# Up-projection of the last three token chunks of an attention-plus-feed-forward kernel by seven block products instead of eight

## The chip, the cores and the metric

The kernel runs on one core of a Trainium2 chip. A core has a matrix engine (TensorE, PE in the profile; its weight loads are listed as PEld), a vector engine (VectorE, DVE), a scalar engine (ScalarE, ACT), GpSimd (POOL) and SyncE (SP), which here only issues transfers. Each engine executes its own queue of instructions in order, and engines wait for each other by semaphores. The metric is device time in microseconds (us) of one execution.

## What is computed

The inputs are q, k and v (8 batches, 8 heads, 576 tokens, 64 elements) and two weight matrices.

```python
scores = scale * np.matmul(q, k.transpose(0, 1, 3, 2))      # scale = 1/8
# heads 0-3: a query sees the last 32 tokens; heads 4-7: every 4th of the last 128
attn = softmax of the masked scores
x = np.matmul(attn, v), heads side by side                   # 4608 tokens x 512
h = x @ w_in                                                 # 512 -> 2048
g = np.maximum(0.01 * h, h)                                  # leaky ReLU
out = g @ w_out                                              # 2048 -> 512, float32
```

## The kernel before

Every engine's order is written by a planner. The kernel makes a list of tasks (`add`, line 68; `dma`, line 74), each with an engine or a choice of engines, an assumed duration and latency, its dependencies and a priority, and `run` (line 85) simulates the engines and sorts the tasks by planned start. The instructions are issued in that order, so each engine's order is fixed when the program is built; at run time an engine waits wherever something it needs is late. Dependencies between instructions are found again from the memory that they touch when the program is built, and become semaphore waits.

**Attention.** Batches are taken in order, two at a time (a pair is `m`). For late batches scores are made on PE (lines 891, 898), the exponential is on ACT (line 910), the mask is a multiplication on DVE (line 924), the product with the values is on PE (line 931), and DVE takes reciprocals and normalizes (lines 949, 953). PE transposes the result (line 979), and ACT or DVE copy it to `xt` (line 560 or 562), which holds x with its 512 features as four blocks of 128 partitions and 1152 tokens of the pair along the free dimension. Tokens stand there in the order of attention's blocks: token 4t + r stands at r times a block length plus t. DVE also transposes q and k (lines 592, 603), and POOL converts and rearranges.

**Feed-forward.** The 4608 tokens are 12 chunks of 384 (`chunks`, line 501), three to a pair: the first 384 tokens of either batch, and the last 192 of both. For the last pair the order is first batch, both remainders, second batch, which are chunks 9, 10 and 11. *Up* (`up`, line 997) makes one of 16 blocks j of 128 hidden units for a chunk: four matmuls (line 1014), one for each 128 input features, with a 128x128 block of w_in as the stationary operand and 384 tokens moving. They add up in one of two PSUM banks (`hps`), and ACT applies the leaky ReLU (Prelu) as it copies the bank to `gt` in float16 (line 1025). *Down* is done plainly for the first 8 tiles of 128 tokens (`down`, line 1055) and for the other 28 in groups of four tiles (`group`, line 1105): a 2x2 block product made of seven block products in place of eight, with sums of blocks of w_out (line 1095) and of g (line 1139) made by DVE, products on PE (line 1153), and results taken out of PSUM by ACT (line 1182) and added by DVE (line 1190). These use the banks `fps`; the last group also uses four others, among them `sps0`, `tp` (called `tpf` in the code) and `ops`, which belong to attention before.

**Stores.** Since the tokens of a chunk are not in their natural order, `rows` (line 1033) splits a tile of 128 tokens into runs whose output rows lie four apart, and `store` (line 1049) issues one transfer for each run on SP's queue. In the last group the second and later runs of a tile go on ACT's queue.

**Order around the change.** An up task's priority comes from the chunk's due time (`begins`, line 506) and j. In the last stage PE alternates ups of chunks 9 to 11 with the down products of the groups. The last up of chunk 11 is followed by the last group alone.

Of the kernel before, what the change touches and what calls it, by code (L numbers as in the profile page):

```python
# [11 lines left out]
AF = mybir.ActivationFunctionType  # L12
ALU = mybir.AluOpType
# [48 lines left out]
class _Plan:  # L62
# [5 lines left out]
    def add(self, eng, dur, lat, deps, fn, prio, soft=0.0, kind=""):  # L68
        choices = eng if isinstance(eng, tuple) else ((eng, dur),)
        t = _Task(choices, lat, deps, fn, prio, soft, len(self.tasks), kind)  # L70
        self.tasks.append(t)
        return t
# [70 lines left out]
def kernel(  # L143
# [10 lines left out]
    nc = tc.nc  # L154
# [3 lines left out]
    B, H, S, D = q.shape  # L158
    assert (B, H, S, D) == (8, 8, 576, 64)
    DM = H * D  # L160
    DFF = moe_w_in.shape[1]
    NP = H // 2
    NI = DM // 128
    NJ = DFF // 128
# [8 lines left out]
    N_UPS = 8  # L173
# [11 lines left out]
    def at(tl, p0, p1, off, *dims):  # L185

        row = tl.ap[0][0]
        return bass.AP(tensor=tl.tensor, offset=tl.offset + p0 * row + off,
                       ap=[[row, p1 - p0]] + [list(d) for d in dims])

    def dram(t, off, *dims):
        return bass.AP(tensor=t.tensor, offset=t.offset + off, ap=[list(d) for d in dims])
# [7 lines left out]
    w_in = sbuf("w_in", [128, NI * DFF])  # L200
    w_out = sbuf("w_out", [128, NJ * DM])
    NST, NNAT, NVS, NV, NT, NE, NR, NO, NG, NL = 5, 3, 3, 3, 6, 4, 4, 3, 3, 2
    PAD = 32
    stg = [sbuf(f"stg{i}", [128, 1152], FP32) for i in range(NST)]
# [4 lines left out]
    vp = [sbuf(f"vp{i}", [128, 12 * 128]) for i in range(NV)]  # L209
    vd = [sbuf(f"vd{i}", [128, 16 * 128]) for i in range(NV)]  # L210
# [9 lines left out]
    xt = [sbuf(f"xt{i}", [128, NI * 1152]) for i in range(2)]  # L220
    gt = [sbuf(f"gt{i}", [128, NJ * 384]) for i in range(NG)]
# [16 lines left out]
    sps0, tpf = bank("sps0"), bank("tp")  # L238
    tpb = tpf.bitcast(FP16)
    ops = [bank(f"ops{i}") for i in range(2)]  # L240
    hps = [bank(f"hps{i}") for i in range(2)]
# [7 lines left out]
    add = plan.add  # L249
# [29 lines left out]
    rings = {}  # L279
# [185 lines left out]
    w_in_t, w_out_t = {}, {}  # L465
# [35 lines left out]
    chunks = [(m, i, 384) for m in range(B // 2) for i in ((0, 1, 2) if m < 3 else (0, 2, 1))]  # L501
# [4 lines left out]
    begins = [0.0]  # L506
# [7 lines left out]
    def columns(c, x, n):  # L514

        i = chunks[c][1]
        if i < 2:
            return S * i + x, [[1, n]]
        return (384 + S * (x // 192) + x % 192,
                [[1, n]] if x % 192 + n <= 192 else [[S, n // 192], [1, 192]])  # L520
# [31 lines left out]
    x_done, x_free = {}, {1: w_used[14] + w_used[15]}  # L552
# [444 lines left out]
    def up(c, j, x, n, done, acc):  # L997

        m, _, n_c = chunks[c]
        x0, dims = columns(c, x, n)  # L1000
        if c == 0 and j in WIDE:
            h_users = []
            ht, name, x_r = {2: (fps[1], "F", -1), 3: (banks["S"][0], "S", -1), 4: (ops[0], "O", 0),
                             5: (ops[1], "O", 1), 6: (tpf, "TP", -1)}[j]
            h_old = rings[name][x_r]
            rings[name][x_r] = h_users
        else:
            hn, h_old = ring("H", len(hps), h_users := [])
            ht = hps[hn]

        def pe(i0, i1):
            def fn(e):
                for i in range(i0, i1):
                    nc.tensor.matmul(ht[:, 0:n],  # L1014
                                     at(w_in, 0, 128, i * DFF + j // 2 * 256 + j % 2, [2, 128]),
                                     at(xt[m % 2], 0, 128, i * 1152 + x0, *dims),
                                     start=(i == 0), stop=(i == NI - 1))
            return fn
        t_p = None
        for i0, i1 in [(i, i + 1) for i in range(NI)] if c == 0 and j in BLOCKS else [(0, NI)]:  # L1020
            t_p = add("PE", (i1 - i0) * (0.0026 + n * 0.000417), 0.25 * (i1 == NI),
                      done + w_in_t[j][:i1] + h_old + [t_p], pe(i0, i1),
                      begins[c] + j * 1.3 - 6.0 * (c == len(chunks) - 1), 0.0, "U")
        t_a = add("ACT", 0.06 + n * 0.00085, 0.22, [t_p] + gt_free.get(c - NG, []),
                  lambda e: nc.scalar.activation(  # L1025
                      out=gt[c % NG][:, j * n_c + x:j * n_c + x + n], in_=ht[:, 0:n],
                      func=AF.Prelu, alpha=0.01),
                  -1000 + c * 16 + j)
        h_users.append(t_a)
        acc[j].append((t_a, x, n))  # L1030
        return t_p

    def rows(c, tt):

        m, i, _ = chunks[c]
        res = []
        for p in range(128):
            x = columns(c, tt * 128 + p, 1)[0]
            for b in (2 * m, 2 * m + 1):
                for u0, nu, base in segs[b]:  # L1040
                    if base <= x < base + 4 * nu:
                        tok = b * S + 4 * (u0 + (x - base) % nu) + (x - base) // nu
            if res and tok == res[-1][1] + 4 * res[-1][2]:
                res[-1][2] += 1
            else:
                res.append([p, tok, 1])
        return res

    def store(ob, i, c, tt, c0, n_o, t_c, users, both=False):
        for n_p, (p0, tok, n) in enumerate(rows(c, tt)):  # L1050
            users.append(load("ACT" if both and n_p else "SP",
                              dram(out, tok * DM + c0, [4 * DM, n], [1, n_o]),
                              ob[p0:p0 + n, i:i + n_o], n, 4 * n_o, [t_c], -3000))

    def down(c, tt, acts, at_time):
# [44 lines left out]
        minus(3, w_block(0, 1), w_block(1, 1), w_block(0, 1), [t_sum[1]] + plain_parts)  # L1100

    last_of = {}
    SUMS = 75.0

    def group(four, acts, at_time, split):

# [14 lines left out]
        if split:  # L1121
            cells = [[(b, 0) for b in pair] for pair in (fps, [sps0, tpf], ops)]
            pairs = ((0,), (1,))
            room = {id(b): last_of[id(b)] for b in fps}
            room.update({id(b): rings["S2"][-1] for b in (sps0, tpf)})
            room.update({id(b): sum(rings["O2"][-2:], []) for b in ops})
        else:
            cells = [[(b, HN * i) for i in range(2)] for b in (*fps, fps[1])]
            pairs = ((0, 1),)
            room = {id(b): last_of.get(id(b), first_banks.get(id(b), [])) for b in fps}  # L1130
        X, Y, Z = cells
# [185 lines left out]
    for m in range(B // 2):  # L1317
        for b in (2 * m, 2 * m + 1):
            if b < EARLY:
                attend(b, 0, *RANKS[2 * b])  # L1320
                if b == 0:
                    release()
                    first_acts = [[] for _ in range(NJ)]
                    first_ups = [up(0, j, 0, 384, x_done[0, 0], first_acts) for j in range(N_UPS)]
                    clear_slots(range(4, NT), -700, x_done[0, 0][-1:])
                    clear_ones((2,), x_done[0, 0][-1:])
                attend(b, 1, *RANKS[2 * b + 1])
            else:
                a, z = WHEN[b - 1], WHEN[b]
                attend(b, None, a, (z - a) / 4)  # L1330
        x_free[m + 2] = first_ups if m == 0 else []
        while n_c < len(chunks) and chunks[n_c][0] == m:
            acts = first_acts if n_c == 0 else [[] for _ in range(NJ)]
            halves = [(0, 192), (192, 192)] if m == 0 and n_c % 3 == 2 else [(0, 384)]
            for i, (x, n) in enumerate(halves):
                x_free[m + 2] += [up(n_c, j, x, n, x_done[n_c, i], acts)
                                 for j in range(0 if n_c else N_UPS, NJ)]
            gt_free[n_c] = []
            all_acts[n_c] = acts
            for i, (c, tt) in enumerate(tiles[:PLAIN]):  # L1340
                if c == n_c:
                    down(c, tt, [[t for t, x, n in a if x < tt * 128 + 128] for a in acts],
                         begins[c + 1] + tt * 6.92 + 0.6)
            if n_c == 2:
                weight_sums()
                half_free[0] = [t for e in (visits[b, vi, 1][1] for b in range(EARLY)
                                            for vi in range(4)) for t in e]
                half_free[0] += sum((visits[1, vi, 1][2] for vi in range(4)), [])
                part_free[0] = part_free[1] = rings["STG"][-1]
                for i in range(2):  # L1350
                    first_banks[id(fps[i])] = rings["F"][i - 2]
            for n, four in enumerate(groups):
                if four[-1][0] == n_c:
                    group(four, all_acts, begins[n_c + 1] + four[-1][1] * 2.0, n == len(groups) - 1)
            n_c += 1
# [59 lines left out]
```

## Time and profile before

| what | us |
|---|---|
| median of 3 runs | 310.16 (309.3 to 310.33) |
| the profiled execution, own time | 311.24 |
| its span, first to last instruction | 309.5 |
| PE busy | 297.8, 96% of the span |
| DVE, ACT, POOL busy | 204.3, 178.7, 126.1 |
| mean granted PE clock | 0.997 |
| last DVE instruction ends | 304.75 |

The profile is of one execution on the chip. The page has the busy time of each engine, the span in 40 slices, the chain of work that ended last, followed back from the last instruction, and the costliest groups of instructions by line, shape and tile. Queries of the trace give further views: a timeline (start, duration, engine, line, operation), waits (who waited for whom, total, times, longest), and windows (busy time of each engine in a stretch). In a group, "gt<-hps 128x384 f16<-128x384 f32 x171" means 171 instructions that write gt from hps with those shapes; behind the bar stand the busy us, the mean ns of one and the idle time before them with what ended it. Times in a timeline count from the start of the span.

### The profile page before, as it was taken

The page shows a single profiled execution, that of the slowest core. Times are in us where ns is not written, and L with a number is a line of the kernel's source. Part 1 is how long each engine was busy: PE and PEld are TensorE (multiplying, and loading weights), DVE is VectorE, ACT ScalarE, POOL GpSimd, SP SyncE. Part 2 cuts the span into 40 slices and gives each one's busy share as a digit, 9 for nine tenths or more (in the row PEclk, how much of TensorE's full clock was granted, in tenths as well). Part 3 has the DMA queues.
Part 4 walks back from the last instruction along what each step waited for, and adds up shares of the span by engine and source line. Part 5 has one row for each costly group of instructions (what it writes and reads, how often), then busy time and mean ns, then how long its engine had stood idle before and what let it go on. Part 6 is the DMA issues. An engine that isn't in the chain of part 4 may idle for free.

```text
span 309.5 us, 7405 instructions
## 1 busy us (share of the span) xinstructions
PE 297.8 (96%) x2795; PEld 214.1 (69%) x2795; DVE 204.3 (66%) x419; ACT 178.7 (58%) x426; POOL 126.1 (41%) x178
## 2 busy tenths in 40 slices
PE   7987999999999999999999999999999999999993
PEld 2534645567777777787777878787887767777882
DVE  5854896689786859969798798967645230070551
ACT  3736775786556678465776665556545655445320
POOL 4449555475675639268645671961000000000000
PEclk9999999999999999999999999999999999999998
DMA  7999998999899999985999978793103010310133
GB/s 245 314 333 401 397 355 152 223 216 222 235 179 221 210 167 192 167 206 123 193 179 181 194 153 193 137 201 80 36 22 84 6 30 2 84 51 2 36 100 105
DMA packets 163188, 51.25 MB, mean 166 GB/s; under 512 B 140752, under 2 KB 160080, under 8 KB 163152
## 3 DMA queue, kind: packets, MB, share of 16 engines
q1 hardware_dynamic: 162128, 50.05, 68.1%
q10 hardware_dynamic: 1024, 0.73, 0.9%
q8 instruction: 22, 0.36, 0.5%
q14 instruction: 14, 0.11, 0.1%
HBM read 41.32 MB, written 9.44 MB: 164 GB/s over the span
## 4 chain that ended last, share of the span: by engine, by line
PE 87%; DMA 4%; DVE 3%; SPq 3%; ACT 1%; issue 1%; DVEq 0%; ACTq 0%
PE hps L1014 38%; PE fps L1153 25%; PE fps L1066 9%; PE ops L931 3%; DMA wst<-in_moe_w_in_dram 3%; SPq L263 3%; PE ops L979 2%; DVE ee L924 1%; DMA stg<-in_k_dram 1%; PE ops L1153 1%; PE tp L610 1%; PE sps L891 1%; PE tp L891 1%; PE sps L898 1%; PE tp L898 1%; ACT gt L1025 1%
## 5 line engine op out<-in xcount | busy, mean ns | idle before, releaser
L1014 PE MATMUL hps<-xt,w_in 128*128 128x384 f16 (+1 forms) x812 | 144.3, 313 | 1.4 <-DVE w_in L273 0.7
L1025 ACT ACTIVATE gt<-hps 128x384 f16<-128x384 f32 (+1 forms) x203 | 93.7, 468 | 69.9 <-PE hps L1014 67.9
L1014 PEld LDWEIGHTS <-w_in 128*128 128x128 f16 x832 | 75.2, 98 | 37.7 <-DVE w_in L273 1.5
L1153 PEld LDWEIGHTS <-gt 128*128 128x128 f16 x672 | 64.7, 98 | 12.0
L597 POOL COPY slots<-turned 64x576 f16<-64x576 f16 x48 | 35.5, 740 | 51.5 <-DVE turned L592 46.8
L1153 PE MATMUL fps<-w_out,gt 128*128 128x256 f16 x416 | 53.6, 273 | 0.0
L273 POOL CAST nat<-stg 128x576 f16<-128x576 f32 (+1 forms) x53 | 38.2, 745 | 7.5 <-DMA stg<-in_q_dram 2.7
L1066 PE MATMUL fps<-w_out,gt 128*128 128x512 f16 x128 | 32.4, 379 | 0.0
L1190 DVE TENSOR_TENSOR osb<-fps,stg 128x512 f32<-128x512 f32 x18 | 12.4, 688 | 28.0 <-ACT stg L1182 19.0
L953 DVE TENSOR_TENSOR rc<-ops,recs 96x384 f16<-96x384 f32 x48 | 25.8, 541 | 0.3
L1182 ACT COPY stg<-fps 128x512 f32<-128x512 f32 (+1 forms) x24 | 12.8, 532 | 13.2 <-PE fps L1153 11.8
L273 POOL CAST vd<-v_all 128x1024 f16<-128x1024 f32 (+2 forms) x20 | 18.0, 918 | 5.5 <-DMA v_all<-in_v_dram 5.3
L949 DVE RECIPROCAL recs<-ops 96x6 f32<-96x6 f32 x48 | 8.9, 185 | 17.2 <-PE ops L931 15.0
L924 DVE TENSOR_TENSOR ee<-ee,con 128x576 f16<-128x576 f16 x24 | 16.7, 699 | 3.8 <-ACT ee L910 3.7
L562 DVE COPY slots<-tp 64x128 f16<-64x128 f16 (+7 forms) x43 | 13.8, 334 | 8.0 <-PE tp L610 7.4
L592 DVE STREAM_TRANSPOSE turned<-nat 128x576 f16<-128x576 f16 x24 | 17.9, 755 | 0.0
L1066 PEld LDWEIGHTS <-gt 128*128 128x128 f16 x128 | 11.5, 98 | 9.1
L603 DVE STREAM_TRANSPOSE slots<-nat 128x576 f16<-128x576 f16 x24 | 17.6, 749 | 0.0
L924 DVE TENSOR_TENSOR el<-el,con 128x576 f16<-128x576 f16 x24 | 15.7, 656 | 2.1 <-ACT el L910 2.1
L273 POOL CAST vp<-v_all 128x768 f16<-128x768 f32 x16 | 15.4, 970 | 3.3 <-DMA v_all<-in_v_dram 2.1
L1139 DVE TENSOR_TENSOR gt<-gt 128x1024 f16<-128x1024 f16 x19 | 12.9, 692 | 3.8 <-PE fps L1153 3.7
L776 ACT ACTIVATE ee<-sps 128x384 f16<-128x384 f32 x20 | 9.8, 490 | 8.6 <-PE sps L770 5.7
(120 smaller groups left out, 399.6 us busy)
## 6 DMA issues: line engine op xcount, KB each, us to landing
stg<-in_q_dram SPq DMA_DIRECT2D x48, 144.0 KB, 3.8
stg<-in_k_dram SPq DMA_DIRECT2D x48, 144.0 KB, 2.9
v_all<-in_v_dram SPq DMA_DIRECT2D x24, 256.0 KB, 3.5
v_all<-in_v_dram SPq DMA_DIRECT2D x24, 192.0 KB, 2.9
gt<-in_moe_w_in_dram SPq DMA_DIRECT2D x5, 512.0 KB, 8.1
out_dram<-osb SPq DMA_DIRECT2D x24, 96.0 KB, 2.0
out_dram<-osb SPq DMA_DIRECT2D x36, 48.0 KB, 1.8
out_dram<-osb SPq DMA_DIRECT2D x25, 64.0 KB, 2.1
```

The costliest lines, as they stand in the source:

```text
L273: ENG[e].tensor_copy(out=dst, in_=src)
L562: nc.vector.tensor_copy(out=dst, in_=src)
L592: lambda e: nc.vector.transpose(xb, na[:, 0:S]), prio)
L597: lambda e, p0=p0, hh=hh: nc.gpsimd.tensor_copy(out=at(qb, p0, p0 + 64, hh * S + o, *od), in_=at(xb, p0, p0 + 64, i, *id_)), prio, 0.0, "m ...
L603: lambda e: nc.vector.transpose(kb[:, PAD:PAD + S], na[:, S:2 * S]), prio)
L924: nc.vector.tensor_tensor(out=x, in0=x, in1=mk, op=ALU.mult)
L953: nc.vector.tensor_tensor(out=at(xb, 0, 96, 768 * n + 64 * i, [256, 3], [128, 2], [1, D]), in0=at(ot, 0, 96, 0, [130, 3], [65, 2], [1, D]) ...
L1014: nc.tensor.matmul(ht[:, 0:n], at(w_in, 0, 128, i * DFF + j // 2 * 256 + j % 2, [2, 128]), at(xt[m % 2], 0, 128, i * 1152 + x0, *dims), st ...
L1025: lambda e: nc.scalar.activation(out=gt[c % NG][:, j * n_c + x:j * n_c + x + n], in_=ht[:, 0:n], func=AF.Prelu, alpha=0.01),
L1066: nc.tensor.matmul(ft, g[:, j * n_c + tt * 128:j * n_c + tt * 128 + 128], w_out[:, j * DM:j * DM + DM], start=(j == 0), stop=(j == NJ - 1))
L1139: lambda e: nc.vector.tensor_tensor(out=dst, in0=a, in1=b, op=op),
L1153: nc.tensor.matmul(bk[:, x:x + HN], tl[:, off + j * step:off + j * step + 128], rhs(j), start=first and x == 0 and j == 0, stop=j == HJ - ...
```

## The change

Chunks 9, 10 and 11 (`FAST`) are projected up by `up_fast` in place of `up`. Their product x times w_in is seen as 2x2 blocks: input features in two halves k, hidden units in two halves n, tokens in two halves y of 192. A quarter p takes two j of either half of the hidden units (four blocks j in all, of 16), and makes its eight block products by seven, each of four matmuls of 192 columns (two j, two input blocks).

- `w_in_sums` makes four sums of blocks of w_in on DVE: three go to `vd`, whose values are no longer needed, and the fourth overwrites a block of w_in after the last plain up.
- For each chunk four differences of blocks of x are made on DVE (`less`) in a slot of `vp`.
- A quarter uses two banks, X and Y, of a ring of three pairs: `hps`; `sps0` and `tp`; `ops`. Products 1, 6, 5 and 3 add up in X, with a copy of X to a slot of `stg` by ACT or DVE (`evict`) after each of the first three. Products 2, 7 and 4 are made in Y, and DVE adds Y to a copy (`plus`).
- Each of the four results goes through the leaky ReLU on ACT (`relu`), three of them from the copies in `stg` and one from X. It writes g in token order: the elements of a residue are written four apart.
- `rows` gives such chunks their natural token order, so a tile has one run, or two where it crosses from one batch's remainder to the other's.

```diff
+    def up_fast(c, done, acc):
+            up_ring.append([[(hps[0], hps[1]), rings["H"][-1] + rings["H"][-2]],
+                            [(sps0, tpf), rings["S2"][-1]],
+                            [ops, rings["O2"][-1] + rings["O2"][-2]]])
...
+        less(1, b(0, 1), b(0, 0), done + old)
+        less(2, b(1, 1), tx[1], [t_x[1]])
+        less(3, b(1, 1), b(0, 1), done + old)
+        less(4, b(1, 0), tx[2], [t_x[2]])
...
+            def product(k, lhs, rhs, cell, first, deps):
+                def pe(e):
+                    for z in range(2):
+                        for i in range(2):
+                            nc.tensor.matmul(cell[:, n * z:n * z + n], lhs(2 * p + z, i), rhs(i),
+                                             start=first and z == 0 and i == 0,
+                                             stop=z == 1 and i == 1, skip_group_check=True)
...
+            p1 = product(0, raw(0, 0), x_raw(0, 0), X, True, done + w_all + room)
+            p2 = product(1, raw(1, 0), x_raw(1, 0), Y, True, done + w_all + room)
+            e1 = evict(0, [p1] + room_k)
+            a11 = plus(0, [e1, p2])
+            r11 = relu(keep[0], 0, 0, [a11])
+            p6 = product(2, summed(1), x_sum(2), X, False, [e1, t_x[2], w_in_sum[2]])
+            p7 = product(3, raw(0, 1), x_sum(3), Y, True, [a11, t_x[3], w_in_sum[3]])
+            e2 = evict(1, [p6] + room_k)
+            p5 = product(4, summed(0), x_sum(1), X, False, [e2, t_x[1], w_in_sum[1]])
+            e4 = evict(2, [p5] + room_k)
+            a22 = plus(2, [e4, p7])
+            r22 = relu(keep[2], 1, 1, [a22])
+            p3 = product(5, summed(2), x_raw(1, 1), X, False, [e4, w_in_sum[4]])
+            p4 = product(6, raw(1, 1), x_sum(4), Y, False, [a22, t_x[4]])
+            r12 = relu(X[:, 0:2 * n], 0, 1, [p3])
+            a21 = plus(1, [e2, p4])
+            r21 = relu(keep[1], 1, 0, [a21])
...
     def rows(c, tt):
+        if c in FAST:
+            x = tt * 128
+            if i < 2:
+                return [(0, (2 * m + i) * S + x, 128, 1)]
...
-            users.append(load("ACT" if both and n_p else "SP",
-                              dram(out, tok * DM + c0, [4 * DM, n], [1, n_o]),
+                              dram(out, tok * DM + c0, [step * DM, n], [1, n_o]),
...
+    SUMS, IN_SUMS = 75.0, 190.0
+    FAST = (9, 10, 11)
...
+                if n_c in FAST:
+                    up_fast(n_c, x_done[n_c, i], acts)
+                    continue
```

## Prediction

> **What bounds the kernel now.** I read the page first: the share of busy time by engine, the slices, and the chain that ended last.
>
> ```profile
> span 309.5 us, 7405 instructions
> PE 297.8 (96%) x2795; PEld 214.1 (69%) x2795; DVE 204.3 (66%) x419; ACT 178.7 (58%) x426; POOL 126.1 (41%) x178
> PE 87%; DMA 4%; DVE 3%; SPq 3%; ACT 1%; issue 1%; DVEq 0%; ACTq 0%
> ```
>
> TensorE (PE) carries 87% of the chain, but a busy PE may still be a waiting one. So next came the waits of PE alone from 180 us on, where the change lies. There is one entry:
>
> ```profile
> PE ops L931 <- DVE ee L924: 0.2, 1, 0.2
> ```
>
> From 180 us to its last matmul PE has 0.2 us of waits: there the end moves by what PE's columns cost. The same stretch by windows (after the span: busy PE, PEld, DVE, ACT, POOL, then clock, DMA share, GB/s):
>
> ```profile
> 222.00:236.00 14.00, 14.00 (x144) 11.01 (x143) 5.29 (x12) 7.44 (x18) 0.00 (x0) 1.00 0.14 40
> 236.00:289.00 53.00, 53.00 (x406) 38.42 (x405) 14.41 (x25) 27.51 (x56) 0.00 (x0) 1.00 0.12 31
> 304.50:309.50 5.00, 0.00 (x0) 0.00 (x0) 0.25 (x1) 0.00 (x0) 0.00 (x0) 0.81 0.24 66
> ```
>
> VectorE (DVE) is 27% and ScalarE (ACT) 52% busy in the stage that changes, at clock 1.00. After PE's last matmul come 5 us of stores. The unit costs are in the timeline of PE and the groups by form (busy us, then mean ns of one):
>
> ```profile
> 74.35 1.03 PE L1066 MATMUL fps<-w_out,gt 128*128 128x512 f16 x4
> 75.21 0.82 PE L1014 MATMUL hps<-xt,w_in 128*128 128x192 f16 x8
> 75.87 0.41 PE L931 MATMUL ops<-vd,el 128*128 128x65 f16 x8
> ...
> 242.28 1.04 PE L1153 MATMUL fps<-w_out,gt 128*128 128x256 f16 x8
> 243.15 1.46 PE L1014 MATMUL hps<-xt,w_in 128*128 128x384 f16 x8
> ...
> 244.45 1.04 PE L1153 MATMUL fps<-w_out,gt 128*128 128x256 f16 x8
> ```
> ```profile
> L1025 ACT ACTIVATE gt<-hps 128x384 f16<-128x384 f32 x171 | 83.8, 492 | 62.4 <-PE hps L1014 60.4
> L848 ACT ACTIVATE rc<-rc 64x384 f32<-64x384 f32 x8 | 4.0, 516 | 0.1
> L1190 DVE TENSOR_TENSOR v_all<-ops,stg 128x256 f32<-128x256 f32 x4 | 1.7, 425 | 3.9 <-ACT stg L1182 3.0 <-PE ops L1153 0.9
> L1095 DVE TENSOR_TENSOR wst<-w_out 128x2048 f16<-128x2048 f16 x1 | 1.2, 1212 | 0.0
> ```
>
> Matmuls are pipelined, so a matmul's cost is the distance of starts: eight of 384 columns take 244.45-243.15 = 1.30 us (0.1625 each), eight of 256 take 0.87 (0.109), and eight of 192, with the same strided w_in weights as the new products, 75.87-75.21 = 0.66 (0.0825). Half the columns cost half the time.
>
> **The change, part by part**, against the profiled execution's own 311.24 us (span 309.5 and 1.74 around it; 1.08 over the median 310.16 of the runs).
>
> *Products.* Removed: 3 chunks x 16 j x 4 = 192 matmuls of 384 columns, 192 x 0.1625 = 31.2 us. Added: 3 x 4 quarters x 7 products x 4 = 336 of 192 columns, 27.7 us. All on PE's path: -3.5. Here a rule speaks against the change. The Trainium skill, "TensorE: Matmul & The Clock Gate", Back-to-back issue gap, gives sustained pairs of weight load and matmul about 81 ns at 128 columns and 131 ns at 512; drawn straight between, my estimate from that page is 89 and 114 ns, so 30.0 us in place of 21.9, 8 us slower. This trace differs: four of 512 columns take 0.86 us (215 ns each, 74.35 to 75.21). I take the rows.
>
> *A gap that goes.* In the chain by time, 32 plain up matmuls follow each other with nothing between:
>
> ```profile
> 249.84 5.47 PE hps L1014 x32
> ```
>
> 5.47 against 32 x 0.1625 = 5.20: PE waits 0.27 us there for ACT to free one of two banks. That run of instructions is gone: -0.27 (0 if a like gap returns).
>
> *The chain through a bank.* Products 1, 6, 5, 3 of a quarter add up in one bank X, and after the first three ACT copies X out before the next may be added. From a product's last issue to the next one's start: drain 0.165 (a 192-column matmul shows 0.246 against 0.0825 of issue), a copy of 384 columns 0.49 (L1025), semaphore 0.05 (DVE L924 ended 197.83, PE went on at 197.88): 0.70 us, 36 times. PE executes in order, so a late copy holds up everything queued behind it. I walked PE's new order by these durations, with the queues of ACT (starts 0.39 apart when back to back: 228.70 to 229.09) and DVE beside it. A dense place, the third and fourth quarter of chunk 9 (t = 0 at product 6 on ops): ops p6 0, hps p1 0.33, hps p2 0.66, ops p7 0.99, ops p5 1.32, hps p6 1.65. The ops copy is done at 0.33+0.70 = 1.03, 0.29 before it is needed; the hps copy starts behind it and is done at 1.42, 0.23 before. Elsewhere down products of 0.87 us lie between and the margins are 0.2 to 1 us; I found none below 0.1. Load of the whole stage, from the first new product to the last: PE 84 x 0.33 + 23 x 0.875 + 0.7 of attention = 48.5 us; ACT 48 relus + 34 copies + 8 down evictions + 1, about 37 us (77%); DVE 36 additions, 2 copies, 8 differences and its down work, about 38 us (78%). Taken: +0.2. Bounds: 0, and 36 x 0.30 = 10.8 if each copy finds most of another ACT instruction in front of it.
>
> *Relus.* 36 of 48 now read SBUF: L848 (SBUF) 516 ns against 486 for the same shape from PSUM (L846), 0.03 more, and within the margins. They write with a step of 4 elements, which no ACT row shows. Bounds: 0.516, and, if a stepped element took two slots, 0.16 + 2 x 0.32 = 0.80 (the slope from 256 to 512 columns, 372 to 586 ns, is 0.84 ns an element). I take 0.516, the nearest row. The Trainium skill, "SBUF — State Buffer", Door 1, says that two hits in a 16-byte line keep full rate, which a step of 8 bytes gives; no run here shows it.
>
> *Sums.* Four w_in sums on DVE, 1.21 each (L1095), 4.9 us, and four differences of 384 for chunk 9, about 0.3 each. They stand before and between the last attention work of DVE (mask, reciprocal, normalization), and the order moves the last score and value matmuls (L898, L931) and a key transposition (L603) behind other PE work. Cover: DVE idles 14.00-5.29 = 8.7 us in 222 to 236, and PE has plain ups and down products; by rows, the first values after a sum are needed 1 to 2 us after they are there. Taken: 0; if the cover were gone, up to 4.9. One wait is new. The second weight load of the first product is made to wait for the fourth sum, though it reads other columns. That sum starts 0.16 us before the last plain up group stops issuing and takes 1.21; PE has 0.875 + 0.08 of other work: +0.2 (0 to 1.2).
>
> *Room and temporaries.* Six banks and slots of stg, vp and vd come free from attention long before; the walk shows no wait for them beyond those above.
>
> *Stores.* Chunks 9 to 11 give 24 store DMAs fewer, and ACT's queue issues none. Before, SP's last store was issued at 306.3, although its data were ready at 304.75:
>
> ```profile
> SPq L263 <- DMA out_dram<-v_all: 2.3, 1, 2.3
> SPq L1410 <- DMA out_dram<-v_all: 1.5, 1, 1.5
> ```
>
> SP waited 2.3 us for a DMA semaphore still held by a store of ACT's queue, and then 1.5 for the landing. With eight stores, each on a semaphore whose last user is long done, the last is issued 0.1 after its data: 306.3-304.85 = 1.45 less. Its 128 rows land a little later than 64 (96 KB median 2.0 against 64 KB 2.1, but 3.1 at worst): I take -1.3, bounds -1.5 and 0.
>
> *Sum:* -3.5 - 0.27 + 0.2 + 0.2 - 1.3 = -4.7, so 306.5 for an execution like the profiled one; from the median 310.16 that is **305.5**.
>
> **The rivals.**
>
> *Copies queue behind relus (slower).* ACT is in order. In the dense quarters it has about 7 instructions x 0.39 = 2.7 us for 2.3 us of PE, so a copy can find a relu, itself waiting for a DVE addition, in front. At 0.30 us a copy, +10.8: 310.2-4.9+10.8 = 316.1. It decides from 4.9/36 = 0.14 us a copy. For it: the 0.27 us above, where two banks alone held PE up; the step-4 write at 0.80. Against: margins of 0.23 and more, 77% load. Chance 0.15.
>
> *Part of it.* Copies cost 0.05 to 0.11 each (1.8 to 4 us), or the relus' stepped write fills ACT in the dense places: 307.2 to 309.2. Chance 0.14. At 0.11 to 0.16 a copy nothing is left: 0.08.
>
> *The tail stays.* If the last 128-row store lands 1.3 us later than a short one, 306.8. Inside the likeliest case.
>
> *The products don't run at half time,* so the change doesn't do what it says: 336 x 0.0929 equals the old 31.2. Against it stand the 192-column rows; a run of more than eight is not in the trace. Chance 0.03, in the slower and equal cases.
>
> **How the numbers follow.** Likeliest: 304.3 to 307.2 (the sum, with 0 to 1.7 us of waits and a tail of 0 to -1.5, and the runs' spread of 1 us), 0.63. With the partial case, faster 0.77. Within 0.3% (0.93 us, about what three runs can tell): 0.08. Slower 0.15. The range reaches from 304.0 into the partial and equal cases, to 310.6; above it lie the slower case and a little of the equal one.
>
> **What would show it.** Right: products of 192 columns 0.33 us apart in fours; waits of PE below 1 us after 230 us; relus at 0.5 us; the last store issued at once; PE's last matmul 3 to 3.8 us earlier. Wrong: an entry of PE waiting for ACT copies of several us, relus near 0.8, or PE waiting for the DVE sums between 220 and 240.

## The result: 2.6% slower, and the profile after

The changed kernel takes 318.2 us (median of 4 runs, 317.8 to 318.7) against 310.25 for the kernel before in the same comparison: ratio 1.026, 95% interval 1.0226 to 1.0293. The forecast was 305.5, with a range to 310.6. The profiled execution took 318.7 us with a span of 316.9, 7.4 more than before.

From the page of the changed kernel: the span, the busy time by engine, PE and ACT in 40 slices of 7.9 us, and the chain that ended last.

```profile
span 316.9 us, 7768 instructions
PE 298.1 (94%) x2939; PEld 223.4 (71%) x2939; DVE 229.1 (72%) x473; ACT 210.2 (66%) x460; POOL 133.1 (42%) x178
...
PE   8887999999999999999999999999999676978996
...
ACT  3635875785557678366776674565549999899721
...
PE 75%; ACT 12%; DMA 4%; SPq 3%; DVE 3%; issue 2%; DVEq 0%; ACTq 0%
```

ACT had 1% of the chain and now has 12%. The slices say where: from the 31st to the 37th ACT stands at 9 tenths (8 in one), and from the 32nd to the 37th PE falls to 6 to 8 (9 in one). That is the stage with the new products. Its groups of relus by form, and then the waits of PE from 180 us to the end (total, times, longest), where before there was one entry of 0.2:

```profile
L1135 ACT ACTIVATE gt<-stg 128x384 f16<-128x384 f32 x36 | 37.2, 1100 | 0.5 <-DVE stg L1129 0.5
L1135 ACT ACTIVATE gt<-sps 128x384 f16<-128x384 f32 x4 | 4.4, 1106 | 0.0
L1135 ACT ACTIVATE gt<-hps 128x384 f16<-128x384 f32 x4 | 4.3, 1078 | 0.0
L1135 ACT ACTIVATE gt<-ops 128x384 f16<-128x384 f32 x4 | 4.2, 1057 | 0.0
```
```profile
PE ops L1112 <- ACT stg L1122: 4.1, 3, 1.8
PE hps L1112 <- ACT stg L1122: 3.1, 3, 2.2
PE sps L1112 <- ACT stg L1122: 2.0, 3, 1.0
PE fps L1294 <- ACT stg L1323: 0.4, 1, 0.4
```

A relu takes 1.06 to 1.11 us, from PSUM as from SBUF, where the old one of the same shape took 0.49. And PE waits for the copies out of bank X. The chain by time shows how the two belong together (start, duration, what):

```profile
250.39 0.33 PE sps L1112 x4
250.72 0.34 PE tp L1112 x4
251.06 0.45 ACT stg L1122
251.51 0.99 ACT gt L1135
252.50 0.32 ACT stg L1122
252.82 0.65 ACT gt L1135
253.47 0.03 issue
253.50 1.11 ACT gt L1135
254.60 0.32 ACT stg L1122
254.92 0.96 ACT gt L1135
```

Between two copies lies a relu; the next product waits for the copy, and the copy for the relu. PE is in the chain only at the top of this stretch, with its products at 0.33 us for four, as forecast. The same stage in windows (busy PE, PEld, DVE, ACT):

```profile
236.70:250.00 13.30, 10.91 (x128) 10.06 (x128) 9.03 (x22) 11.98 (x20) 0.00 (x0) 1.00 0.08 22
250.00:262.00 12.00, 9.37 (x97) 8.12 (x95) 6.66 (x15) 12.00 (x19) 0.00 (x0) 1.00 0.06 17
262.00:274.00 12.00, 9.92 (x99) 8.91 (x99) 5.93 (x11) 11.82 (x20) 0.00 (x0) 1.00 0.03 8
274.00:286.50 12.50, 10.35 (x115) 9.82 (x113) 7.61 (x15) 11.12 (x18) 0.00 (x0) 1.00 0.20 58
286.50:299.00 12.50, 11.58 (x117) 10.52 (x116) 6.95 (x13) 10.72 (x17) 0.00 (x0) 1.00 0.07 23
```

PE is busy 52.1 of 62.3 us and ACT 57.6. PE misses 10.2 us there, at clock 1.00 throughout.

The theory after the result: a float16 result written 4 elements (8 bytes) after the one before it costs ACT more than twice the time. Back to back the relus started 0.76 to 0.86 us apart, most of them above 0.8, where contiguous instructions of that size start 0.37 to 0.39 apart, so by estimate 48 x 0.45 = 21.6 us more work on ACT, which then is the bound. Rivals: the source or the shape of the access pattern costs the time, not the write; the chain through the bank costs it whatever a relu takes; the step is harmless except together with the copies.

### The profile page after: what moved, and what is told of

Its sections match the earlier page's. It is cut to its first block, busy times and chain, and to the rows that moved or that the text cites. A ratio compares the mean times of both kernels' runs of the same rounds, so it can differ in the third digit from the quotient of the medians.

```text
span 316.9 us, 7768 instructions
## 1 busy us (share of the span) xinstructions
PE 298.1 (94%) x2939; PEld 223.4 (71%) x2939; DVE 229.1 (72%) x473; ACT 210.2 (66%) x460; POOL 133.1 (42%) x178
## 4 chain that ended last, share of the span: by engine, by line
PE 75%; ACT 12%; DMA 4%; SPq 3%; DVE 3%; issue 2%; DVEq 0%; ACTq 0%
PE hps L1014 28%; PE fps L1294 22%; PE fps L1206 9%; ACT gt L1135 8%; PE ops L931 3%; DMA wst<-in_moe_w_in_dram 3%; SPq L263 3%; ACT stg L1122 2%; PE ops L979 2%; PE ops L1112 1%; DMA stg<-in_k_dram 1%; PE ops L1294 1%; PE tp L610 1%; PE sps L891 1%; PE tp L891 1%
## 5 line engine op out<-in xcount | busy, mean ns | idle before, releaser
L1014 PE MATMUL hps<-xt,w_in 128*128 128x384 f16 (+1 forms) x620 | 109.0, 309 | 1.5 <-DVE w_in L273 0.8
L1025 ACT ACTIVATE gt<-hps 128x384 f16<-128x384 f32 (+1 forms) x155 | 70.2, 461 | 51.9 <-PE hps L1014 50.3
L1014 PEld LDWEIGHTS <-w_in 128*128 128x128 f16 x640 | 56.6, 98 | 27.6 <-DVE w_in L273 1.5
L273 POOL CAST nat<-stg 128x576 f16<-128x576 f32 (+1 forms) x53 | 39.4, 770 | 9.8 <-DMA stg<-in_k_dram 3.7
L1135 ACT ACTIVATE gt<-stg 128x384 f16<-128x384 f32 x36 | 37.2, 1100 | 0.5 <-DVE stg L1129 0.5
L273 POOL CAST vp<-v_all 128x768 f16<-128x768 f32 x16 | 20.6, 1291 | 7.0 <-DMA v_all<-in_v_dram 3.5
L1112 PEld LDWEIGHTS <-vd 128*128 128x128 f16 x144 | 12.6, 98 | 11.6 <-issue 11.3
L924 DVE TENSOR_TENSOR el<-el,con 128x576 f16<-128x576 f16 x24 | 14.9, 622 | 3.3 <-ACT el L910 3.2
L1112 PEld LDWEIGHTS <-w_in 128*128 128x128 f16 x192 | 16.3, 98 | 0.9 <-issue 0.5
```

The lines of the kernel that those rows point to most:

```text
L273: ENG[e].tensor_copy(out=dst, in_=src)
L924: nc.vector.tensor_tensor(out=x, in0=x, in1=mk, op=ALU.mult)
L1014: nc.tensor.matmul(ht[:, 0:n], at(w_in, 0, 128, i * DFF + j // 2 * 256 + j % 2, [2, 128]), at(xt[m % 2], 0, 128, i * 1152 + x0, *dims), st ...
L1025: lambda e: nc.scalar.activation(out=gt[c % NG][:, j * n_c + x:j * n_c + x + n], in_=ht[:, 0:n], func=AF.Prelu, alpha=0.01),
L1112: nc.tensor.matmul(cell[:, n * z:n * z + n], lhs(2 * p + z, i), rhs(i), start=first and z == 0 and i == 0, stop=z == 1 and i == 1, skip_gr ...
L1135: lambda e: nc.scalar.activation(out=at(g, 0, 128, j * n_c + w * y, [n_c, 2], [1, n_r], [4, n // n_r]), in_=at(src, 0, 128, 0, [n, 2], [n ...
```

## Experiments

**Contiguous writes, and the stores apart.** The relu writes its results side by side. The first kernel also goes back to the old stores; the second keeps one store per tile.

```diff
-    out=at(g, 0, 128, j * n_c + w * y, [n_c, 2], [1, n_r], [4, n // n_r]),
-    in_=at(src, 0, 128, 0, [n, 2], [n // n_r, n_r], [1, n // n_r]),
+    out=at(g, 0, 128, j * n_c + n * y, [n_c, 2], [1, n]),
+    in_=at(src, 0, 128, 0, [n, 2], [1, n]),
```

> The changed kernel, but the leaky ReLU of a quarter writes its 384 results side by side, in attention's token order, and the stores of chunks 9 to 11 go back to the runs of before. All tasks and their planned costs stay, so the order of work is the one after the change. Theory 'write step' (ACT is the bound because a write of 2-byte elements 8 bytes apart takes 1.1 us in place of 0.5; the relus started 0.83 to 0.86 us apart back to back, so 48 x 0.45 = 21 us of ACT): relus fall to 0.49 to 0.55 us, PE's waits for ACT copies fall from 9 us to below 1 us, and the time to 306 to 308 us (products and gap of my sum, the tail of before). Rival 'chain through a bank' (each copy waits behind other ACT work whatever a relu takes): relus fall, but PE still waits several us for ACT copies and the time stays above 311. Rival 'source' (three of four relus read SBUF): relus from the copies stay near 1.1 us and the time at 315 to 318.

> As the first run of this set, with the one store per output tile of the changed kernel; the output rows of chunks 9 to 11 are then left in the wrong order, so token order is what it leaves out. It prices the stores alone: the span after the last DVE instruction was 4.75 us before the change and 2.6 after it. If the stores give that by themselves, this run is 1.3 to 2.2 us faster than the first, at 304 to 306.5; if the tail was short only because the last group ended differently, it equals the first within 0.5 us.

Measured: 306.12 (ratio to before 0.9863, with its 95% interval, 0.9827 to 0.99) with the old stores, 305.22 (0.9839, 0.98 to 0.9877) with one store per tile. Relus of the first by form, and the waits of PE from 180 us on:

```profile
L1135 ACT ACTIVATE gt<-stg 128x384 f16<-128x384 f32 x36 | 18.4, 529 | 2.0 <-DVE stg L1129 1.8
L1135 ACT ACTIVATE gt<-hps 128x384 f16<-128x384 f32 x4 | 2.0, 498 | 0.0
```
```profile
PE ops L931 <- DVE ee L924: 0.2, 1, 0.2
```

With the same tasks at the same planned costs, the waits for copies are gone and so are 12 us. The second kernel shows the same relus and the same single wait; it differs from the changed kernel in the relus alone, and 13.0 us lie between the two (318.2 and 305.22). The source costs 0.03 us, as the prediction had it from line 848; the chain through the bank costs nothing by itself with relus of 0.5 us. The stores are 0.9 us apart in the medians, with intervals that overlap: less than the 1.3 to 2.2 of the one expectation and more than the 0.5 of the other. In the two profiled executions the span ends 2.9 and 2.65 us after the last DVE instruction, so the stores' tail differs by 0.2 us only.

**Token order by the read.** The same results in the same places, with the loops nested the other way: neighbours are written one after another, and the source is read with jumps.

```diff
-    out=at(g, 0, 128, j * n_c + w * y, [n_c, 2], [1, n_r], [4, n // n_r]),
-    in_=at(src, 0, 128, 0, [n, 2], [n // n_r, n_r], [1, n // n_r]),
+    out=at(g, 0, 128, j * n_c + w * y, [n_c, 2], [4, n // n_r], [1, n_r]),
+    in_=at(src, 0, 128, 0, [n, 2], [1, n // n_r], [n // n_r, n_r]),
```

> The changed kernel with token order kept, but the loops of the leaky ReLU nested the other way: it reads 2 (chunks 9 and 11) or 4 (chunk 10) tokens from as many residues, 384 or 192 bytes apart in float32, and writes those 2 or 4 results side by side. The number of dimensions is that of the changed kernel. Theory 'write step': the cost follows the distance of successive writes, so relus of chunk 10 fall to 0.5 to 0.6 us and those of chunks 9 and 11, with every second write adjacent, to 0.5 to 0.85; time 305 to 312. Rival 'shape' (three free dimensions, or a permutation as such, cost the time): all stay at 1.0 to 1.1 us and the time at 316 to 319.

Measured: 306.94 (0.9897, 0.9864 to 0.993). By form, over the whole stage:

```profile
L1135 ACT ACTIVATE gt<-stg 128x384 f16<-128x384 f32 x36 | 24.8, 713 | 1.1 <-DVE stg L1129 1.1
L1135 ACT ACTIVATE gt<-sps 128x384 f16<-128x384 f32 x4 | 2.0, 510 | 0.4 <-PE sps L1112 0.4
```

From PSUM the jumps cost next to nothing (0.50 to 0.51 us by form, 0.49 to 0.50 contiguous). From SBUF a relu took 0.60 to 0.63 us where it reads from two places and, in chunk 10, 0.85 to 0.97 where it reads from four. Three dimensions and a permutation are not what cost the time, so "shape" falls. The expectation had chunk 10 cheapest, since its writes are fully adjacent; it is the dearest, because jumps in an SBUF source have a price of their own.

**Other write steps.** Two columns apart in all chunks, then three; and one run with 3, 8 and 16 in chunks 9, 10 and 11.

```diff
-    out=at(g, 0, 128, j * n_c + w * y, [n_c, 2], [1, n_r], [4, n // n_r]),
+    out=at(g, 0, 128, j * n_c + y, [n_c, 2], [2, n]),                          # step 2
+    out=at(g, 0, 128, j * n_c + n * y, [n_c, 2], [1, 3], [3, n // 3]),          # step 3
+    out=at(g, 0, 128, j * n_c + w * y, [n_c, 2], [1, n_r], [step, n // n_r]),   # 3, 8, 16
```

> The changed kernel with relus that write every second column (4 bytes apart; the two token halves interleave), two free dimensions, source in order; token order is left out. Theory 'write step' by distance: between 0.5 and 1.1, some 0.7 to 0.8 us, time 308 to 313; if any step other than 1 costs the full price, 1.1 us and 316 to 319. Rival 'shape': 0.5 us, as two dimensions are those of before, and 304 to 307.

> The changed kernel with another write step of the relus in each chunk: 3 elements (6 bytes) in chunk 9, 8 elements (16 bytes) in chunk 10, 16 elements (32 bytes) in chunk 11; source in order; token order is left out. It prices the step beside 1 (0.49 us), 2 (0.61) and 4 (1.06 to 1.10). If the cost follows the number of results that share a short line, step 3 lies between 2 and 4 at 0.8 to 0.9 us and the cost is level from 4 on, 1.1 us at 8 and 16. If it goes on growing with the distance, 8 and 16 take 2 us or more, and the time goes above 330.

> The changed kernel with relus written 3 elements apart in all three chunks, 0.81 to 0.88 us each and 0.62 to 0.65 from start to start: about the upper bound that the prediction gave a relu (0.80). One store per tile, token order left out. Theory 'ACT is full' (time is lost only beyond the point where ACT's work exceeds PE's 49.8 us of the stage): ACT had 38.5 us there with contiguous relus, plus 48 x 0.24 = 50, just full, and so 306 to 309. Rival 'each relu counts' (the time follows the relu from step 2 to step 4 in a straight line): 305.9 + (0.83 - 0.61) / (1.08 - 0.61) x 12.3 = 311.7, 310.5 to 313.

Relus from the copies with step 2, then with step 3 in all chunks, then a stretch of chunk 11 in the third kernel, with step 16:

```profile
L1135 ACT ACTIVATE gt<-stg 128x384 f16<-128x384 f32 x36 | 22.2, 648 | 1.5 <-DVE stg L1129 1.3
```
```profile
L1135 ACT ACTIVATE gt<-stg 128x384 f16<-128x384 f32 x36 | 29.4, 863 | 0.6 <-DVE stg L1129 0.5
```
```profile
L1136 ACT ACTIVATE gt<-stg 128x384 f16<-128x384 f32 x8 | 15.2, 2021 | 0.2 <-DVE stg L1129 0.2
```

| step (elements of 2 bytes) | one relu, us | kernel with one store per tile, us |
|---|---|---|
| 1 | 0.49 to 0.53 | 305.2 (306.1 with the old stores) |
| 2 | 0.61 to 0.65 | 305.9 |
| 3 | 0.81 to 0.88 | 310.7 |
| 4 (the change) | 1.06 to 1.11 | 318.2 |
| 8 | 1.8 to 2.2 | not comparable: mixed steps |
| 16 | 1.8 to 2.2 | in one run, 340.3 |

The price grows from step to step up to 8 elements and is the same at 16. The expectation that it is level from 4 on was wrong: 8 costs nearly twice what 4 does. The step, not the shape, sets the price: step 2 has the two dimensions of the old pattern and still costs 0.12 us, and steps 3, 8 and 16 have the three dimensions of the changed kernel and cost less or more than it. Step 2 was cheaper than "by distance" had it: 0.61 to 0.65 us in place of 0.7 to 0.8, and a time that lay where "shape" expected it.

Step 3 also tells how the kernel's time follows. A relu there costs what the prediction took as its upper bound (0.80), and the kernel is the same as before: 1.0017 (0.9992 to 1.0043). "ACT is full" over the whole stage gave 306 to 309 and is refuted in that form; the straight line from step 2 to step 4 gave 310.5 to 313, and 310.7 lies in that. But from step 1 to step 2 the medians differ by 0.7 us only, with intervals that overlap, so no straight line through all four is shown. The windows of the step 3 kernel show where it does:

```profile
236.70:250.00 13.30, 12.42 (x150) 11.74 (x148) 10.46 (x25) 12.29 (x24) 0.00 (x0) 1.00 0.10 28
250.00:262.00 12.00, 10.28 (x107) 9.11 (x105) 7.56 (x15) 12.00 (x24) 0.00 (x0) 1.00 0.02 6
262.00:274.00 12.00, 12.00 (x131) 11.33 (x129) 6.88 (x13) 9.56 (x18) 0.00 (x0) 1.00 0.20 55
274.00:286.50 12.50, 11.66 (x121) 10.68 (x119) 9.80 (x18) 12.25 (x22) 0.00 (x0) 1.00 0.10 34
```

PE loses 1.7 us in the second row, where ACT is full, 0.9 and 0.8 in the first and fourth, where ACT is at 92% and 98%, and nothing in the third, where ACT still idles 2.4 us. ACT fills by stretches.

**The step alone, in the kernel before.** Eight products, old stores, and the relus of the plain ups of chunks 9 to 11 written 4 apart.

```diff
-    out=gt[c % NG][:, j * n_c + x:j * n_c + x + n], in_=ht[:, 0:n],
+    out=(at(gt[c % NG], 0, 128, j * n_c, [1, 4], [4, 96]) if c > 8 else
+         gt[c % NG][:, j * n_c + x:j * n_c + x + n]),
+    in_=at(ht, 0, 128, 0, [96, 4], [1, 96]) if c > 8 else ht[:, 0:n],
```

> The kernel before, eight products, where the relus of the plain ups of chunks 9 to 11 write 4 elements apart in place of side by side; stores as before, so token order is left out. It does one part of the change alone. Theory 'write step': relus of 128x384 written with step 4 take 1.05 to 1.1 us in PE's shadow only where PE gives them time. An up takes PE 0.65 us and a relu starts 0.84 us after the one before it, so in PE's run of eight ups (5.2 us) 1.3 to 1.6 us are lost, and ACT has about 27.5 + 48 x 0.45 = 49 us in a stage of 53: slower by 1 to 5 us, 311 to 315. Rival 'only together' (the step costs nothing without the copies and additions of the seven-product form): 309.5 to 310.8.

Measured: 312.76 (1.0078, 1.0051 to 1.0104), 2.4 us over before. Most of the relus in the stage (43 of 48), and a wait of PE that the kernel before did not show:

```profile
L1025 ACT ACTIVATE gt<-hps 128x384 f16<-128x384 f32 x43 | 41.1, 1067 | 5.6 <-PE hps L1014 5.4
```
```profile
PE hps L1014 <- ACT gt L1025: 1.0, 3, 0.5
```

The same price, 1.07 us, without any copy, so "only together" falls. It costs 2.4 us here and 13 in the changed kernel. PE's timelines of the two profiled executions show where 2.3 us are lost here: 0.4 in the pairs of ups before the run of eight ups, 1.8 in that run, which takes 7.30 us in place of 5.47, and nothing after it, where at most two ups stand between down products, though the relus there are as long. That fits the load: before this edit ACT was 52% busy in the stage, while in the changed kernel with contiguous relus it is at 77% already.

**The stores alone, in the kernel before.** The rows of the changed kernel for chunks 9 to 11, so one store per tile and none on ACT's queue.

```diff
+        if c > 8:
+            x = tt * 128
+            if i < 2:
+                return [(0, (2 * m + i) * S + x, 128)]
...
-                              dram(out, tok * DM + c0, [4 * DM, n], [1, n_o]),
+                              dram(out, tok * DM + c0, [(1 if c > 8 else 4) * DM, n], [1, n_o]),
```

> The kernel before with the output rows of chunks 9 to 11 of the changed kernel, one store per tile (token order is left out) and none on ACT's queue: the store part alone. My step priced it at -1.3 us, bounds -1.5 and 0. By it: 308.7 to 309.2, and a span of 2.5 to 3.5 us after the last DVE instruction in place of 4.75. Rival: the 4.75 of the profiled execution was its own wait, and others of the kernel before end sooner (the first run with contiguous relus and the old stores showed 2.9): the same as before within 0.5 us.

Measured: 309.61 (0.9973, 0.9951 to 0.9996), so -0.8 us, -1.5 to -0.1, between the two expectations; the interval reaches both. Two of SP's waits near the end:

```profile
SPq L1416 <- DMA out_dram<-v_all: 1.2, 1, 1.2
...
SPq L263 <- ACT v_all L1188: 0.4, 1, 0.4
```

SP's wait of 2.3 us, which the prediction put down to a store of ACT's queue, is gone, and the span ends 2.6 us after the last DVE instruction (4.75 before). But with the new up-projection and contiguous relus the old stores end 2.9 us after it as well. Why the old stores wait less there is open.

**The planner told the price.** One number: a relu is planned at 0.85 us.

```diff
-                t = add("ACT", 0.06 + 2 * n * 0.00085, 0.22, deps + g_old,
+                t = add("ACT", 0.85, 0.22, deps + g_old,
```

> The changed kernel, instructions unchanged, with a relu planned at 0.85 us (the distance at which they started) in place of 0.386, so that the planner can put copies on DVE and order the queues for it. Relus stay at 1.1 us. Theory 'ACT is full': 48 x 0.85 + 9 x 0.58 + 0.7 = 47 us of ACT without any copy, and DVE had 38 of 50; with the copies shared both are full at about 50 to 53 us, so most of the 12 us between stepped and contiguous relus comes back: 307 to 313. Rival 'chain' (the relus in front of a result hold the next step up whatever the sharing): 315 to 318.

Measured: 308.69 (0.9951, 0.9929 to 0.9972), 9.5 us below the changed kernel and a little faster than before. Relus cost what they did (1.11 to 1.14 us). The planner moved copies to DVE, 17 of 36 in place of 2:

```profile
L1124 DVE COPY stg<-ops 128x384 f32<-128x384 f32 x8 | 4.4, 550 | 0.5 <-PE ops L1112 0.5
L1124 DVE COPY stg<-sps 128x384 f32<-128x384 f32 x6 | 3.3, 550 | 0.3 <-PE sps L1112 0.2
...
L1124 DVE COPY stg<-hps 128x384 f32<-128x384 f32 x3 | 1.6, 550 | 0.0
```

So 9.5 of the 13.0 us between stepped and contiguous relus (both with one store per tile), nearly three quarters, came from queues that were written for a relu of 0.386 us; how much of that is the sharing of copies and how much the order was not taken apart. "Chain", which expected 315 to 318, falls.

**A version that beats both.** Contiguous relus and old stores in chunks 9 and 10; in chunk 11, most of the last group, pairs are written side by side and tiles are stored whole. Beside it the first kernel of this section once more.

```diff
+    out=(at(g, 0, 128, j * n_c + 2 * y, [n_c, 2], [4, n // 2], [1, 2]) if c == 11 else
+         at(g, 0, 128, j * n_c + n * y, [n_c, 2], [1, n])),
+    in_=(at(src, 0, 128, 0, [n, 2], [1, n // 2], [n // 2, 2]) if c == 11 else
+         at(src, 0, 128, 0, [n, 2], [1, n])),
...
-        if c in FAST:
+        if c == 11:
```

> Contiguous relus in chunks 9 and 10 with the stores of before; in chunk 11, which holds three of the last group's four tiles, token order by writing the two tokens of a half side by side and reading the source 384 bytes apart (0.50 us from PSUM, 0.62 from the copies), and one store per tile. If the end of the stores is what separated the two runs with contiguous relus (0.9 us), this kernel takes it without any waits of PE: 305.0 to 305.8, 0.3 to 1.0 below the run with contiguous relus in this set. If that difference was run spread, the two are equal within 0.3 us.

> The kernel with contiguous relus and the stores of before once more, on the chip of this set, as the level for the other two: 305.5 to 306.7.

Measured: 305.84 (0.9851, 0.9822 to 0.988) and 306.33 (0.9879, 0.9844 to 0.9914). They are 1.5% and 1.2% faster than before, and both write the output in its right order; the 0.5 us between them is within their intervals, so what storing whole tiles gives here is not settled. The windows of the second, over its stage:

```profile
234.70:248.00 13.30, 13.26 (x162) 12.73 (x161) 12.09 (x28) 11.38 (x27) 0.00 (x0) 1.00 0.11 29
248.00:260.00 12.00, 12.00 (x133) 11.47 (x131) 7.77 (x15) 10.44 (x25) 0.00 (x0) 1.00 0.04 11
260.00:272.00 12.00, 12.00 (x133) 11.45 (x131) 8.69 (x16) 8.29 (x20) 0.00 (x0) 1.00 0.25 67
272.00:284.50 12.50, 12.50 (x131) 11.68 (x129) 8.18 (x15) 8.49 (x19) 0.00 (x0) 1.00 0.09 23
```

PE is full, and ACT has 38.6 us in 49.8. It is not even: 86% and 87% in the first two rows, 69% and 68% in the others.

## Why the prediction was wrong, step by step

**The step that failed: Relus.** "I take 0.516, the nearest row", between 0.516 and 0.80. Measured: 1.06 to 1.11. The row of line 848 has the shape and the source right (0.53 with contiguous writes), but not the one property that was new, the step. The upper bound was no bound: "if a stepped element took two slots" chose a factor, and no row limited it. A price that no row shows needs an upper end from a mechanism, or a rival of its own with the point from which it decides. The kernel with step 3 gives that point: at about 0.85 us a relu the change is worth nothing, in queues planned as these are. The rule on two hits in a 16-byte line, quoted beside this step from the Trainium skill, "SBUF — State Buffer", Door 1, would keep the full rate here; the runs show 2.1 to 2.3 times the contiguous duration for this write, and the measurement decides.

**The load that hid it.** "ACT ... about 37 us (77%)" is the average over the stage. It is right (38.6 with contiguous relus), but the first 25 us are at 86%, and the stepped relus make it 57.6 us of work, 19.0 more, for a stage that takes 49.6 with contiguous ones. The prediction had a warning of its own in "2.7 us for 2.3 us of PE" in the dense quarters, worked out with the short relu. The partial case, "the relus' stepped write fills ACT in the dense places: 307.2 to 309.2", named the mechanism; its price was too small, because 0.80 was the limit, and because even relus of 0.81 to 0.88 us gave 310.7.

**The rival that came.** "Copies queue behind relus (slower)" described what the trace shows, down to PE's waits for L1122. It priced 0.30 us a copy and 316.1. Measured: the stage from the first new product to the last lasts 62.3 us (236.52 to 298.48 and 0.33) against 49.6 with contiguous relus, 12.7 more, or 0.35 for each of 36 copies. Its chance of 0.15 leaned on margins of 0.23 us that were computed with the wrong relu.

**What held.** The rest of the sum: the kernel with contiguous relus and everything else of the change took 305.22, 5.1 us below the kernel before in its set, against the forecast of 305.5 and -4.7. Part of that agreement is luck: with the old stores it is already -4.2 (-5.4 to -3.1), where the sum without its term for the stores gives -3.4, and the -1.3 for the stores did not come out in that size. Part by part:

- *Products.* Four of 192 columns take 0.33 us in stretches without waits, so "not at half time" falls. The estimate from the Trainium skill, "TensorE: Matmul & The Clock Gate", Back-to-back issue gap, 89 ns at 192 columns, would be 0.36 for four; these rows show 0.33, and they decide.
- *The chain through a bank.* Forecast +0.2, measured 0 with relus of 0.5 us (PE waits for no copy); with relus of 1.1 us this is where PE waits.
- *Sums.* No wait for them but the one named: the first product's four matmuls stretch over 0.71 us in place of 0.49, +0.22 against +0.2, for its second weight load waits 0.3 us for the fourth sum. Line 1 below is that product, line 2 an undisturbed one, both from PE's timeline in the changed kernel:

```profile
236.52 0.71 PE L1112 MATMUL sps<-xt,w_in 128*128 128x192 f16 x4
...
237.72 0.49 PE L1112 MATMUL tp<-xt,w_in 128*128 128x192 f16 x4
```

- *Stores.* -1.3 forecast; alone -0.8 (-1.5 to -0.1) in time and -2.1 in the profiled tail. In size uncertain: behind the new up-projection the old stores end 2.9 us after the last DVE instruction, not 4.75, and that tail is then only 0.2 us longer than with one store per tile.

## What to carry to other kernels

When a reorder is folded into an instruction that runs anyway, price the new access pattern by itself before trusting the row of the same shape; here it cost more than the saved products (13.0 us against 3.5), and the same order cost 1.7 us when neighbours were written together (306.94 against 305.22, with intervals that just overlap). Look at the load of an engine stretch by stretch, for an average of 77% hid a half of the stage at 86%. And where a planner writes the queues, a wrong duration in it can cost more than the slow instruction does: telling it the true one brought back 9.5 of 13.0 us.

## What the runs showed of the hardware that was not expected

- An ACT instruction of 128x384 that writes float16 to SBUF takes 0.49 to 0.53 us contiguous, 0.61 to 0.65 with step 2, 0.81 to 0.88 with step 3, 1.06 to 1.11 with step 4, and 1.8 to 2.2 with steps 8 and 16. From the start of one relu to that of the next it is 0.61 to 0.66 us at step 3, 0.76 to 0.86 at step 4 and 1.34 to 1.71 at 8 and 16. With steps 8 and 16 level, this looks as if the price went by the pieces of 16 bytes that are written, 144, 192 and 384 of them: the longest distances come to about 4.5 ns a piece (an estimate from these figures). Four results a piece come close to the full rate: 0.12 us more at step 2, and 0.50 us from PSUM where pairs lie side by side, every 8 bytes. Whether bytes or elements count was not tried.
- Reading float32 in another order costs ACT next to nothing from PSUM (0.50 to 0.51 us). From SBUF, where reading in order takes 0.53, it takes 0.60 to 0.63 from two places and 0.85 to 0.97 from four.
